# Dense products in column tiles, and score blocks outside score runs

## Chip, cores and metric

The kernel runs on one core of one Trainium2 chip. The metric is the device time of one execution in microseconds (us), given as the median of three runs. A core has TensorE (PE; its weight loads are shown as PEld), VectorE (DVE), ScalarE (ACT), GpSimd (POOL) and SyncE (SP), each with its own instruction queue; they wait for one another by semaphores. TensorE writes PSUM, which here holds eight banks of 128 partitions x 512 fp32.

## What is computed

```python
xn = layernorm(x)                                   # x: 2048 x 512, bf16
q = (xn @ wq).reshape(B, S, 32, 16).transpose(0, 2, 1, 3)
k, v = xn @ wk, xn @ wv                             # 16 wide, shared by all 32 heads
p = softmax(einsum("bhqd,bkd->bhqk", q, k) * 0.25)
s = (einsum("bhqk,bkd->bhqd", p, v) heads side by side) @ wo
g = silu(silu(xn @ w1) @ w2)                        # w1: 512 x 1792, w2: 1792 x 512
out = x + s * g
```

## The kernel before

The queries are cut into 4 chunks of 512, the heads into 8 groups of 4, the keys into 16 tiles of 128. So there are 32 groups in all (chunk by chunk), each with 16 key tiles of 4 rows, a row being one head. One row of one key tile is a **block**: scores of 128 keys x 512 queries, one PSUM bank. There are 2048.

**Scores** (`score`, `burst`, L523 to L544). A head has 16 dimensions, so TensorE is used in four row tiles of 32 partitions: up to four blocks are computed side by side, head i from partitions 32i. Keys lie in `kTa` for even groups, and shifted by 16 partitions in `kTb` for odd ones.

**Exponentials.** ScalarE takes two blocks at once from a double bank `psA` (`exp_A`, L560: 128x1024, then two rows of one key tile are done). VectorE takes single blocks, or a pair, from the banks D and D1 (`psD`) or F (`psF`): it makes an int16 that read as bf16 is a power of two (`exp_D`, L582). Three versions of it, shifted by constants, are averaged for accuracy; the other two come from GpSimd, which adds the constants for a whole tile of four blocks (`shift`, L607). The second buffer set for these lies in parts of `x_sb`.

**Attention times values** (`emit_PV`, L650). Here TensorE is used in four column tiles: a **quad** is four products with 128 keys to 32 outputs each, one per row of the group, into `psO`. A block of ScalarE needs one product, a block of VectorE three. At the end of a group VectorE normalises (`gn1` to `gn4`).

**Dense work** (`emit_job`, L901): q, the two layers of the gate (h and z), and the output product (w, and wp for the last chunk). It uses the whole array, 128x128 weights and 512 columns, always into `psF`. h and z go through a tanh on ScalarE (L939) and a product on VectorE (L971). For a token tile, z leaves the gate in `tmp_sb` (two sets of four); `w` multiplies it into `fin_sb` (L983), and `add` adds x into `ob_sb` (L950), which is stored.

**Order.** All engines' instructions are put in order by a planner when the kernel is built (the loop at L1180). It models each engine (`Sched.model`, L95): a product of 512 columns 0.216 us, a switch between row, column and full mode 0.104 us. It goes from **score run** to score run: a run is two blocks for ScalarE and, in the other two row tiles, blocks for VectorE if its banks are free (`score_run`, `fill_D`). `needed` is the latest start with which ScalarE won't wait, `release` the earliest. Between runs lies a gap with a number of slots of 0.216 us, each used for a quad or a dense product; if both stand in one gap, a slot is given up for the switch (L1218, L1220). Slots that stay empty can get products of zeros (`filler`, L917, and `warm`, L334) that keep TensorE's clock up, if its recent activity is below KEEP. Dense jobs have a fixed order by due time (`timed`, L766 to L773) and are paced by `behind`. Which blocks VectorE takes is not fixed: a key tile is opened for VectorE when a bank is free in a run and nothing else is open, and ScalarE takes what is left. The exponentials of ScalarE are as many as remain.

A tile for ScalarE takes rows 0, 1 in one run and 2, 3 in another; VectorE's blocks in a run are of the other two rows. VectorE's tiles are taken from a group's last key tiles. Finished exponentials of ScalarE lie in a ring of 11 buffers (`pa_sb`) until their products are done.

In `Sched`, `reads` and `writes` give the waits: whatever isn't done yet is waited for by a semaphore.

Of the kernel before, what the change touches and what calls it, by code (L numbers as in the profile page):

```python
# [13 lines left out]
P = 128  # L14
# [182 lines left out]
def bass_recurrent_scan__grouped_kv_mqa__dense_activation_silu__prompt_kernel(  # L197
# [33 lines left out]
    AGE2, AGE_ST, FIRST, FRONT_D, FRONT_K, SHORT, ST_EARLY, Q_ACT = 12.0, 1.5, 9.4, 1, 4, 0, 3, 1  # L231
    KEEP, ENDQ, ROUND, MAXJOB, AHEAD, Q_EARLY = 0.6, 12, 3.0, 2, 3, 0.20
    LEAD, LEAD_END, SLIP, AGE, AGE1, MARGIN = 3, 3, 0.2, 2.0, 1.2, 0.0
    HALF_LO, HALF_HI = 1, 3
    EV = "vava"
    PVWAIT = 0.2
    NF, F_FROM, F_LEFT, F_LATE, DENSE_END, HOLD, F_BEHIND = 14, 0.05, 9, 3, 0.95, 10, 0

    with ExitStack() as es:
# [13 lines left out]
        w2_sb = sb("w2_sb", [P, NFT, D])  # L253
        kT_sb = [sb("kTa_sb", [P, S]), sb("kTb_sb", [P, S])]
        vaug_sb = sb("vaug_sb", [P, 1 + NPH, NKT, 32])
        qT_sb = sb("qT_sb", [P, 2, NDC, NQ])
# [6 lines left out]
        t_sb = sb("t_sb", [P, 2, NQ])  # L263
        tmp_sb = sb("tmp_sb", [P, 2, 4, D])
        fin_sb = sb("fin_sb", [P, 2, D])
        ob_sb = sb("ob_sb", [P, NOB, D])
# [562 lines left out]
        def front_evac(tk):  # L829
# [36 lines left out]
        def emit_job(t, n):  # L866
# [31 lines left out]
            def f(e):  # L898
                for m in items:
                    l, r = pair(m)  # L900
                    h = e.matmul(ap, lhsT=l, rhs=r, start=(m == 0), stop=(m == end))  # L901
                return h
            op("pe", f, reads=rd, writes=[b], cost=("full", [None] * len(items), NQ))
            jst["part"] += len(items)
            if k != "wp":
                jst["slots"] += len(items)
            if jst["part"] == SIZE[k]:
# [3 lines left out]
                else:  # L911
                    task(k, evac, 0.69, jb=jb, bank=b, reads=[b], writes=[])
                if k in ("z", "w"):
# [3 lines left out]
        def filler(n):  # L917
            gi = state["g"]
            if gi < NGRP and K.pe_last >= gdone[gi] and all(npv[gi]):
                def f(e):  # L920
                    for _ in range(n):
                        r = e.matmul(psO[:, :], lhsT=zero_sb[:, 0:P], rhs=zero_sb[:, :], start=False, stop=False,
                                     skip_group_check=True)
                    return r
                op("pe", f, reads=["zero"], writes=["O"], cost=("full", [None] * n, NQ))
                return
# [29 lines left out]
        def add(tk):  # L956
            tt = tk["jb"][1]
            final_add("v", tt, fin_sb[:, tt % 2, :], ("fin", tt % 2))
            tok.add(("add", tt))

        def evac(tk):
# [3 lines left out]
            if k in ("h", "z"):  # L965
# [3 lines left out]
                else:  # L969
                    dst, key = tmp_sb[:, (jb[1] // 4) % 2, jb[1] % 4, :], ("tmp", jb[1] % 8)  # L970
                op("v", lambda e: e.scalar_tensor_tensor(out=dst, in0=t_sb[:, n % 2, :], scalar=1.0, in1=src,  # L971
# [9 lines left out]
            elif k == "w":  # L981
                tt = jb[1]
                op("v", lambda e: e.scalar_tensor_tensor(out=fin_sb[:, tt % 2, :], in0=src, scalar=0.25,  # L983
                                                         in1=tmp_sb[:, (tt // 4) % 2, tt % 4, :],
                                                         op0=ALU.mult, op1=ALU.mult),
                   reads=[b, ("tmp", tt % 8)], writes=[("fin", tt % 2)], cost=tk["cost"])
                tok.add(("wev", tt))
                task("add", add, 0.42, jb=jb, reads=[("fin", tt % 2), ("x", 12 + tt % 4)], writes=[])
            elif k == "wp":
# [71 lines left out]
        def v_cand():  # L1061
# [4 lines left out]
            if blks and may_D(blks):  # L1066
# [3 lines left out]
                if len(two) == 2 and (two[0]["bank"], two[1]["bank"]) == ("D", "D1") and two[0]["idx"] == two[1]["idx"] and may_D(two):  # L1070
                    d2 = max(tv, K.ready("v", ["D", "D1"], [ph_key(0, slot_of[b["idx"]], b["pos"]) for b in two]))
                    if d2 <= d + 0.1 and meets(d + 0.735) >= meets(d2 + 1.27):
                        d, blks = d2, two
# [41 lines left out]
        def score_run(t):  # L1115
# [18 lines left out]
            if second:  # L1134
                ast["tile"] = None

        def fill_D(t, free):
# [42 lines left out]
        while state["g"] < NGRP or front or jobs or jst["open"] or tasks:  # L1180
# [23 lines left out]
            if slots > 0:  # L1204
                gi = state["g"]
                full = blocked or sum(held(("pa", k)) for k in range(NPA)) >= HOLD
# [6 lines left out]
                can = job_ready(t) and not did  # L1213
                end = gi < NGRP and t >= gdone[gi] - PVWAIT and owed[gi] <= ENDQ
                dense_first = can and not full and not end and (jst["open"] or behind() or not more)
# [30 lines left out]
        half = [(slice(256 * h, 256 * h + 256), ("half", h)) for h in range(2)]  # L1246
        tmp = tmp_sb[:, (tt // 4) % 2, :, :]
        def resid(k, src, key, start):
# [32 lines left out]
        def gate(k):  # L1281
            bank, key = tail_bank(k)
            op("v", lambda e: e.scalar_tensor_tensor(out=fint_sb[:, k, :], in0=bank, scalar=0.25, in1=tmp[:, k, :],
                                                     op0=ALU.mult, op1=ALU.mult),
               reads=[key, ("tmp", (tt + k) % 8)], writes=[("spart", k)], cost=0.69)

        def gate_late(k):
            op("v", lambda e: e.tensor_tensor(fint_sb[:, k, :], fint_sb[:, k, :], tmp[:, k, :], ALU.mult),
               reads=[("spart", k), ("tmp", (tt + k) % 8)], writes=[("spart", k)], cost=0.42)

# [49 lines left out]
```

## Time and profile before

| what | us |
|---|---|
| median of 3 runs (lowest, highest) | 679.59 (679.39, 679.68) |
| profiled execution, its time | 679.43 |
| its span, first to last instruction | 677.6 |
| first exponential of ScalarE ends at | 11.74 |
| last exponential of ScalarE ends at | 668.54 |

A group line of the profile reads: line, engine, operation, output <- inputs, shapes, xcount, then busy time and mean ns of one, then the idle time in front of these instructions and what ended it. In the timeline a row has start, duration, engine, line, and in brackets the idle time before it. The granted clock of TensorE was 1.00 throughout. Instructions on ScalarE and VectorE overlap a little with the next one, so the distance of their ends, not their duration, is what one costs.

### The profile page before, as it was taken

The page shows a single profiled execution, that of the slowest core. Times are in us where ns is not written, and L with a number is a line of the kernel's source. Part 1 is how long each engine was busy: PE and PEld are TensorE (multiplying, and loading weights), DVE is VectorE, ACT ScalarE, POOL GpSimd, SP SyncE. Part 2 cuts the span into 40 slices and gives each one's busy share as a digit, 9 for nine tenths or more (in the row PEclk, how much of TensorE's full clock was granted, in tenths as well). Part 3 has the DMA queues.
Part 4 walks back from the last instruction along what each step waited for, and adds up shares of the span by engine and source line. Part 5 has one row for each costly group of instructions (what it writes and reads, how often), then busy time and mean ns, then how long its engine had stood idle before and what let it go on. Part 6 is the DMA issues. An engine that isn't in the chain of part 4 may idle for free.

```text
span 677.6 us, 14816 instructions
## 1 busy us (share of the span) xinstructions
PE 637.9 (94%) x6232; PEld 186.8 (28%) x6311; DVE 594.2 (88%) x994; ACT 664.0 (98%) x762; POOL 366.6 (54%) x371
## 2 busy tenths in 40 slices
PE   8999999999999999999999999999999999999997
PEld 4422222222222222222222222222222222222222
DVE  7888888888898879988898898998988889988997
ACT  6999999999999999999999999999999999999995
POOL 3154644644655646655565555646464646765563
PEclk9999999999999999999999999999999999999999
DMA  6340000000000001000000000000000000000100
GB/s 175 135 145 2 1 1 1 1 2 1 1 1 2 1 16 32 18 1 1 1 2 1 2 1 2 16 17 17 18 1 1 1 2 2 1 1 17 48 1 32
DMA packets 12322, 12.25 MB, mean 18 GB/s; under 512 B 2528, under 2 KB 11744, under 8 KB 12256
## 3 DMA queue, kind: packets, MB, share of 16 engines
q1 hardware_dynamic: 11680, 10.78, 5.1%
q8 instruction: 49, 0.80, 0.5%
q10 hardware_dynamic: 576, 0.52, 0.2%
q14 instruction: 17, 0.14, 0.1%
HBM read 8.95 MB, written 2.10 MB: 16 GB/s over the span
## 4 chain that ended last, share of the span: by engine, by line
ACT 89%; PE 4%; DVE 4%; issue 1%; POOL 1%; DMA 0%; POOLq 0%; SPq 0%
ACT pa_sb L560 84%; ACT t_sb L939 5%; PE psA L531 1%; PE psO L650 1%; DVE stats_sb L346 1%; DVE ph_sb L582 1%; DVE xn_sb L367 1%; PE psF L901 1%; DMA x_sb<-in_A_x_dram 0%; POOL ph_sb L607 0%; POOL rstd_sb L355 0%; PE psD L378 0%; DVE kTa_sb L421 0%; DVE x_sb L582 0%; PE psD L531 0%
## 5 line engine op out<-in xcount | busy, mean ns | idle before, releaser
L560 ACT ACTIVATE pa_sb<-psA 128x1024 bf16<-128x1024 f32 x677 | 641.2, 1177 | 1.7 <-PE psA L531 1.2
L607 POOL INT64_ADD ph_sb<-ph_sb x292 | 302.5, 1048 | 234.8 <-DVE ph_sb L582 234.7
L582 DVE TENSOR_SCALAR ph_sb<-psD 128x512 int16<-128x512 f32 x530 | 360.1, 690 | 52.4 <-PE psD L531 43.9
L650 PE MATMUL psO<-ph_sb,vaug_sb 128*32 128x512 bf16 x1758 | 211.7, 384 | 0.6 <-ACT pa_sb L560 0.3
L650 PE MATMUL psO<-pa_sb,vaug_sb 128*32 128x512 bf16 x1354 | 199.2, 384 | 0.0
L531 PE MATMUL psA<-qT_sb,kTa_sb 32*128 32x512 bf16 x688 | 133.5, 384 | 9.5 <-ACT pa_sb L560 6.2
L531 PE MATMUL psA<-qT_sb,kTb_sb 32*128 32x512 bf16 x666 | 129.2, 384 | 11.5 <-ACT pa_sb L560 9.5
L531 PE MATMUL psD<-qT_sb,kTb_sb 32*128 32x512 bf16 x323 | 118.2, 384 | 0.0
L531 PE MATMUL psD<-qT_sb,kTa_sb 32*128 32x512 bf16 x314 | 116.9, 384 | 0.4 <-DVE ph_sb L582 0.4
L607 POOL INT64_ADD x_sb<-x_sb x54 | 55.7, 1044 | 41.8 <-DVE x_sb L582 41.8
L582 DVE TENSOR_SCALAR x_sb<-psD 128x512 int16<-128x512 f32 (+1 forms) x96 | 66.9, 700 | 12.4 <-PE psD L531 11.7
L531 PEld LDWEIGHTS psA<-qT_sb,kTa_sb 32*128 32x128 bf16 x688 | 32.4, 90 | 140.1 <-ACT pa_sb L560 126.4
L531 PEld LDWEIGHTS psA<-qT_sb,kTb_sb 32*128 32x128 bf16 x666 | 31.3, 91 | 142.0 <-ACT pa_sb L560 132.3
L650 PEld LDWEIGHTS psO<-ph_sb,vaug_sb 128*32 128x32 bf16 x1758 | 53.6, 95 | 56.4 <-issue 37.0
L901 PE MATMUL psF<-xnT_sb,w_sb 128*128 128x512 bf16 x195 | 61.3, 384 | 3.4 <-issue 2.2
L901 PE MATMUL psF<-w_sb,u_sb 128*128 128x512 bf16 x208 | 62.5, 384 | 1.9 <-issue 1.4
L650 PEld LDWEIGHTS psO<-pa_sb,vaug_sb 128*32 128x32 bf16 x1354 | 50.1, 94 | 42.7 <-issue 31.0
L650 PE MATMUL psO<-x_sb,vaug_sb 128*32 128x512 bf16 x324 | 55.6, 384 | 0.0
L939 ACT ACTIVATE t_sb<-psF 128x512 bf16<-128x512 f32 x72 | 54.1, 752 | 0.0
L971 DVE SCALAR_TENSOR_TENSOR u_sb<-t_sb,psF 128x512 bf16<-128x512 bf16 x56 | 38.2, 682 | 7.0 <-ACT t_sb L939 6.4
L582 DVE TENSOR_SCALAR ph_sb<-psF 128x512 int16<-128x512 f32 x48 | 32.4, 676 | 0.0
L531 PEld LDWEIGHTS psD<-qT_sb,kTa_sb 32*128 32x128 bf16 x314 | 27.6, 91 | 2.0 <-DVE ph_sb L582 1.5
(107 smaller groups left out, 343.2 us busy)
## 6 DMA issues: line engine op xcount, KB each, us to landing
w_sb<-in_B_w_dram SPq DMA_DIRECT2D x2, 1792.0 KB, 8.3
x_sb<-in_A_x_dram SPq DMA_DIRECT2D x18, 128.0 KB, 2.2
out_dram<-ob_sb SPq DMA_DIRECT2D x14, 128.0 KB, 1.7
x_sb<-in_A_x_dram SPq DMA_DIRECT2D x3, 512.0 KB, 6.7
wop_sb<-in_A_wo_dram SPq DMA_DIRECT2D x1, 512.0 KB, 4.0
wq_sb<-in_A_wq_dram SPq DMA_DIRECT2D x1, 384.0 KB, 6.4
x_sb<-in_A_x_dram ACTq DMA_DIRECT2D x2, 128.0 KB, 3.0
kTb_sb<-kTa_sb SPq DMA_DIRECT2D x16, 16.0 KB, 1.8
```

Of the source, the lines that this page charges most:

```text
L346: op("v", lambda e: e.bn_stats(stats_sb[:, t, :], x_sb[:, t, :]), reads=[("x", t)], writes=[("st", t)], cost=0.687)
L367: op(eng, lambda e: e.tensor_scalar(xn_sb[:, t % 8, :], x_sb[:, t, :], mv_sb[:, t, 0:1], rstd_sb[:, t:t + 1], op0=ALU.subtract, op1=ALU.mult),
L531: return e.matmul(ap, lhsT=kT_sb[g % 2][32 * i:32 * i + 32, kt * P:(kt + 1) * P], rhs=qT_sb[32 * i:32 * i + 32, c % 2, g // 2, :], start=T ...
L560: d = op("a", lambda e: e.activation(pa_sb[:, sl, :], psA[k][:, :], ACT.Exp, scale=ESCALE), reads=["A%d" % k], writes=[("pa", sl)], cost=2 ...
L582: d = op("v", lambda e: e.tensor_scalar(ph_ap(0, sl, 512 * pos, 512 * pos + m), src, float(PH_ONE + PH_BIAS), 0.0, op0=ALU.add, op1=ALU.ma ...
L607: d = op("gp", lambda e, j=j: e.int64_add(ph_ap(j, sl, 0, 4 * NQ).bitcast(I64), ph_ap(0, sl, 0, 4 * NQ).bitcast(I64), PH_SHIFT[j] * 0x0001 ...
L650: r = e.matmul(psO[32 * i:32 * i + 32, :], lhsT=vaug_sb[:, p["v"], p["kt"], :], rhs=p["ap"], start=s0, stop=s1, tile_position=(0, 32 * i), ...
L901: h = e.matmul(ap, lhsT=l, rhs=r, start=(m == 0), stop=(m == end))
L939: op("a", lambda e: e.activation(t_sb[:, n % 2, :], bank_ap(b), ACT.Tanh, scale=0.5 if jb[0] == "h" else 0.25), reads=[b], writes=[("t", n ...
L971: op("v", lambda e: e.scalar_tensor_tensor(out=dst, in0=t_sb[:, n % 2, :], scalar=1.0, in1=src, op0=ALU.add, op1=ALU.mult), reads=tk["read ...
```

## The change

- **Dense products** are made of four products in column tiles (`columns`), each 128 rows by 32 outputs, to the same bank. The zero products into `psO` are too. In the planner they cost as much as before, and they are now in the same mode as the quads.
- **Masked keys**: a new tensor `km_sb` holds, for rows 2 and 3 (MI), both halves of the key layout and the last 6 key tiles (MK), the keys in that row's partitions and zeros in all others. GpSimd clears it, and SP's queue moves keys into it (`move_KM`, 8 transfers). A score block can then be computed as a product over all 128 rows in column mode, outside of a score run.
- **Filling**: `col_want` asks whether such a block would be at VectorE at least XGAIN = 0.6 us (in a leftover slot XLEFT = 0.5 us) earlier than by riding in the next run, and `col_fill` issues it. The loop that fills the gap asks for every slot anew, and gives no slot up between quads and dense products.
- **Buffers**: `tmp_sb` has one set of four, `fin_sb` is gone and `w` and `add` work in `ob_sb`. A z job therefore waits for the output product of the token tile four before, and the due times are clipped to that order.
- **Constants**: KEEP 0.6 to 0.65, Q_EARLY 0.20 to 0.18, AGE 2.0 to 2.5, DENSE_END 0.95 to 0.96.

```diff
+    MI, MK = (2, 3), 6
+    XHOLD, XGAIN, XLEFT, XBEH, PAIR = 8, 0.6, 0.5, 99, 1
+        km_sb = sb("km_sb", [P, 2, len(MI), MK * P])
-        tmp_sb = sb("tmp_sb", [P, 2, 4, D])
-        fin_sb = sb("fin_sb", [P, 2, D])
+        tmp_sb = sb("tmp_sb", [P, 4, D])
...
+        def columns(e, bank, lhsT, rhs, start, stop):
+            for i in range(4):
+                r = e.matmul(bank[32 * i:32 * i + 32, :], lhsT=lhsT[:, 32 * i:32 * i + 32], rhs=rhs, start=start, stop=stop,
+                             tile_position=(0, 32 * i), skip_group_check=True)
+            return r
...
+        def move_KM(c):
+            a = max(0, (NKT - MK) * P - c * NQ)
+            if a >= NQ:
+                return
+            d0 = c * NQ + a - (NKT - MK) * P
+            for p in range(2):
+                for m, i in enumerate(MI):
+                    op("sp", lambda e, p=p, m=m, i=i: e.dma_start(
+                        km_sb[32 * i + DH * p:32 * i + DH * p + DH, p, m, d0:d0 + NQ - a],
+                        kT_sb[0][32 * i:32 * i + DH, c * NQ + a:(c + 1) * NQ]),
+                       reads=[("kT", 0, 2 * c), ("kT", 0, 2 * c + 1)], writes=[("km", p, m, c)], lane=f"mm{c}{p}{m}")
...
         rstd_pow(1)
+        op("gp", lambda e: e.memset(km_sb[:], 0.0), writes=[("km", p, m, c) for p in range(2) for m in range(len(MI)) for c in range(NC)], cost=2.6)
...
+        when = {jb: x for x, jb in timed}
+        timed = [(min(x, when["z", jb[1] + 4] - 0.001) if jb[0] == "w" else x, jb) for x, jb in timed]
...
-                return all(("hev", c, ft) in tok for ft in range(NFT)) and (c < 2 or ("wev", jb[1] - 8) in tok) and \
+                return all(("hev", c, ft) in tok for ft in range(NFT)) and (c < 1 or ("wev", jb[1] - 4) in tok) and \
...
                     move_K(c)
+                    move_KM(c)
...
-                    h = e.matmul(ap, lhsT=l, rhs=r, start=(m == 0), stop=(m == end))
+                    h = columns(e, ap, l, r, m == 0, m == end)
...
-            op("pe", f, reads=rd, writes=[b], cost=("full", [None] * len(items), NQ))
+            op("pe", f, reads=rd, writes=[b], cost=("col", [0, 1, 2, 3] * len(items), NQ))
...
+        def col_pick(t):
+            for o in dst["open"]:
+                gi, kt = o["tile"]
+                for i in o["todo"]:
+                    if i in MI and kt >= NKT - MK and K.ready("pe", [("km", gi % 2, MI.index(i), kt // 4)]) <= t:
+                        return o, i
+            return None
+
+        def col_want(t, least):
+            if front or group_A() >= NGRP or sum(held(("pa", k)) for k in range(NPA)) >= XHOLD or (XBEH < 99 and behind(XBEH)):
+                return None
+            pick = col_pick(t)
+            if pick is None:
+                return None
+            vfree = K.free["v"] + 0.62 * len(dst["fifo"])
+            ride = needed() + 0.43
+            best = None
+            for b in BANKS:
+                if hold[b] is None and (b != "F" or not jobs or not next_job(t)):
+                    r = max(t, K.ready("pe", [], [b]))
+                    gain = ride - max(vfree, r + 0.43)
+                    if gain > least and (best is None or r < best[0]):
+                        best = (r, b) + pick
+            return best
+
+        def col_fill(w):
+            _, bank, o, i = w
...
+            def f(e):
+                return columns(e, bank_ap(bank), km_sb[:, g % 2, m, k0:k0 + P], qT_sb[:, c % 2, g // 2, :], True, True)
+            op("pe", f, reads=[("qT", c % 2, g // 2), "qTb", ("km", g % 2, m, kt // 4)], writes=[bank], cost=("col", [0, 1, 2, 3], NQ))
+            dst["fifo"].append(dict(tile=o["tile"], i=i, bank=bank, idx=idx, pos=pos, rows=o["rows"]))
...
-                if dense_first:
-                    did = emit_job(t, slots)
-                if slots - did >= (2 if did else 1):
-                    did += emit_PV(max(t, K.pe_last + K.pe_len) + 0.08, slots - did - (1 if did else 0))
-                if can and not dense_first and slots - did >= (2 if did else 1):
-                    did += emit_job(t, slots - did - (1 if did else 0))
+                while did < slots:
+                    t1 = t if not did else max(t, K.pe_next("col"))
+                    w = col_want(t1, XGAIN)
+                    part = slots - did
+                    if w is not None:
+                        k = int((w[0] - t1 - 0.05) / 0.2163 + 0.8)
+                        if k <= 0:
+                            did += col_fill(w)
+                            continue
+                        part = min(part, k)
...
+                    n = 0
+                    if dense_first:
+                        n = emit_job(t1, part)
+                    if not n:
+                        n = emit_PV(t1 + 0.08, part)
+                    if not n and can and not dense_first:
+                        n = emit_job(t1, part)
+                    if not n:
+                        w = col_want(t1, XLEFT)
+                        if w is not None and w[0] <= t1 + 0.1:
+                            n = col_fill(w)
+                        else:
+                            break
+                    did += n
```

More of the change, by code (lines that the diff above doesn't have):

```diff
@@ L231, in bass_recurrent_scan__grouped_kv_mqa__dense_activation_silu__prompt_kernel @@
     AGE2, AGE_ST, FIRST, FRONT_D, FRONT_K, SHORT, ST_EARLY, Q_ACT = 12.0, 1.5, 9.4, 1, 4, 0, 3, 1
-    KEEP, ENDQ, ROUND, MAXJOB, AHEAD, Q_EARLY = 0.6, 12, 3.0, 2, 3, 0.20
-    LEAD, LEAD_END, SLIP, AGE, AGE1, MARGIN = 3, 3, 0.2, 2.0, 1.2, 0.0
+    KEEP, ENDQ, ROUND, MAXJOB, AHEAD, Q_EARLY = 0.65, 12, 3.0, 2, 3, 0.18
+    LEAD, LEAD_END, SLIP, AGE, AGE1, MARGIN = 3, 3, 0.2, 2.5, 1.2, 0.0
     HALF_LO, HALF_HI = 1, 3
@@ L236, in bass_recurrent_scan__grouped_kv_mqa__dense_activation_silu__prompt_kernel @@
     PVWAIT = 0.2
-    NF, F_FROM, F_LEFT, F_LATE, DENSE_END, HOLD, F_BEHIND = 14, 0.05, 9, 3, 0.95, 10, 0
+    MI, MK = (2, 3), 6
+    XHOLD, XGAIN, XLEFT, XBEH, PAIR = 8, 0.6, 0.5, 99, 1
+    NF, F_FROM, F_LEFT, F_LATE, DENSE_END, HOLD, F_BEHIND = 14, 0.05, 9, 3, 0.96, 10, 0
     with ExitStack() as es:
@@ L911, in emit_job @@
                 else:
-                    task(k, evac, 0.69, jb=jb, bank=b, reads=[b], writes=[])
+                    task(k, evac, 0.69, jb=jb, bank=b, reads=[b], writes=[("ob", jb[1] % NOB)] if k == "w" else [])
                 if k in ("z", "w"):
@@ L921, in f @@
                     for _ in range(n):
-                        r = e.matmul(psO[:, :], lhsT=zero_sb[:, 0:P], rhs=zero_sb[:, :], start=False, stop=False,
-                                     skip_group_check=True)
+                        r = columns(e, psO, zero_sb[:, 0:P], zero_sb[:, :], False, False)
                     return r
-                op("pe", f, reads=["zero"], writes=["O"], cost=("full", [None] * n, NQ))
+                op("pe", f, reads=["zero"], writes=["O"], cost=("col", [0, 1, 2, 3] * n, NQ))
                 return
@@ L957, in add @@
             tt = tk["jb"][1]
-            final_add("v", tt, fin_sb[:, tt % 2, :], ("fin", tt % 2))
+            final_add("v", tt, ob_sb[:, tt % NOB, :], ("ob", tt % NOB))
             tok.add(("add", tt))
@@ L969, in evac @@
                 else:
-                    dst, key = tmp_sb[:, (jb[1] // 4) % 2, jb[1] % 4, :], ("tmp", jb[1] % 8)
+                    dst, key = tmp_sb[:, jb[1] % 4, :], ("tmp", jb[1] % 4)
                 op("v", lambda e: e.scalar_tensor_tensor(out=dst, in0=t_sb[:, n % 2, :], scalar=1.0, in1=src,
@@ L982, in evac @@
                 tt = jb[1]
[L983 to L986, printed above, removed]
+                op("v", lambda e: e.scalar_tensor_tensor(out=ob_sb[:, tt % NOB, :], in0=src, scalar=0.25,
+                                                         in1=tmp_sb[:, tt % 4, :], op0=ALU.mult, op1=ALU.mult),
+                   reads=[b, ("tmp", tt % 4)], writes=[("ob", tt % NOB)], cost=tk["cost"])
                 tok.add(("wev", tt))
-                task("add", add, 0.42, jb=jb, reads=[("fin", tt % 2), ("x", 12 + tt % 4)], writes=[])
+                task("add", add, 0.42, jb=jb, reads=[("ob", tt % NOB), ("x", 12 + tt % 4)], writes=[])
             elif k == "wp":
@@ L1071, in v_cand @@
                     d2 = max(tv, K.ready("v", ["D", "D1"], [ph_key(0, slot_of[b["idx"]], b["pos"]) for b in two]))
-                    if d2 <= d + 0.1 and meets(d + 0.735) >= meets(d2 + 1.27):
+                    if PAIR and d2 <= d + 0.1 and meets(d + 0.735) >= meets(d2 + 1.27):
                         d, blks = d2, two
@@ L1135, in score_run @@
                 ast["tile"] = None
+        def col_pick(t):
[23 more added lines that the diff above has]
+            _, bank, o, i = w
+            (gi, kt), idx = o["tile"], o["idx"]
+            c, g = gi // NG, gi % NG
+            pos = len(o["rows"]) - len(o["todo"])
+            o["todo"].remove(i)
+            if not o["todo"]:
+                dst["open"].remove(o)
+            m, k0 = MI.index(i), (kt - NKT + MK) * P
+            def f(e):
+                return columns(e, bank_ap(bank), km_sb[:, g % 2, m, k0:k0 + P], qT_sb[:, c % 2, g // 2, :], True, True)
+            op("pe", f, reads=[("qT", c % 2, g // 2), "qTb", ("km", g % 2, m, kt // 4)], writes=[bank], cost=("col", [0, 1, 2, 3], NQ))
+            dst["fifo"].append(dict(tile=o["tile"], i=i, bank=bank, idx=idx, pos=pos, rows=o["rows"]))
+            hold[bank] = "blk"
+            return 1
         def fill_D(t, free):
@@ L1204, in bass_recurrent_scan__grouped_kv_mqa__dense_activation_silu__prompt_kernel @@
             if slots > 0:
-                gi = state["g"]
-                full = blocked or sum(held(("pa", k)) for k in range(NPA)) >= HOLD
                 jb = next_front(t)
@@ L1212, in bass_recurrent_scan__grouped_kv_mqa__dense_activation_silu__prompt_kernel @@
                         did = 2
-                can = job_ready(t) and not did
-                end = gi < NGRP and t >= gdone[gi] - PVWAIT and owed[gi] <= ENDQ
-                dense_first = can and not full and not end and (jst["open"] or behind() or not more)
-                if dense_first:
-                    did = emit_job(t, slots)
-                if slots - did >= (2 if did else 1):
-                    did += emit_PV(max(t, K.pe_last + K.pe_len) + 0.08, slots - did - (1 if did else 0))
-                if can and not dense_first and slots - did >= (2 if did else 1):
-                    did += emit_job(t, slots - did - (1 if did else 0))
+                while did < slots:
[8 more added lines that the diff above has]
+                        part = min(part, k)
+                    full = blocked or sum(held(("pa", k)) for k in range(NPA)) >= HOLD
+                    can = job_ready(t1) and not (jb and did == 2 and False)
+                    gi = state["g"]
+                    end = gi < NGRP and t1 >= gdone[gi] - PVWAIT and owed[gi] <= ENDQ
+                    dense_first = can and not full and not end and (jst["open"] or behind() or not more)
+                    n = 0
[12 more added lines that the diff above has]
+                    did += n
             if more and not blocked:
@@ L1246, in bass_recurrent_scan__grouped_kv_mqa__dense_activation_silu__prompt_kernel @@
         half = [(slice(256 * h, 256 * h + 256), ("half", h)) for h in range(2)]
-        tmp = tmp_sb[:, (tt // 4) % 2, :, :]
+        tmp = tmp_sb[:, :, :]
         def resid(k, src, key, start):
@@ L1284, in gate @@
                                                      op0=ALU.mult, op1=ALU.mult),
-               reads=[key, ("tmp", (tt + k) % 8)], writes=[("spart", k)], cost=0.69)
+               reads=[key, ("tmp", (tt + k) % 4)], writes=[("spart", k)], cost=0.69)
         def gate_late(k):
             op("v", lambda e: e.tensor_tensor(fint_sb[:, k, :], fint_sb[:, k, :], tmp[:, k, :], ALU.mult),
-               reads=[("spart", k), ("tmp", (tt + k) % 8)], writes=[("spart", k)], cost=0.42)
+               reads=[("spart", k), ("tmp", (tt + k) % 4)], writes=[("spart", k)], cost=0.42)
         for k in (1, 3):
```

## Prediction

> **What bounds the kernel now.** I read the page's busy times first, then the chain that ended last, the groups, the waits, and last the timeline gap by gap. The page shows two nearly full engines:
>
> ```profile
> PE 637.9 (94%) x6232; PEld 186.8 (28%) x6311; DVE 594.2 (88%) x994; ACT 664.0 (98%) x762; POOL 366.6 (54%) x371
> ...
> ACT 89%; PE 4%; DVE 4%; issue 1%; POOL 1%; DMA 0%; POOLq 0%; SPq 0%
> ...
> L560 ACT ACTIVATE pa_sb<-psA 128x1024 bf16<-128x1024 f32 x677 | 641.2, 1177 | 1.7 <-PE psA L531 1.2
> ```
>
> ScalarE carries the chain, and in front of its 677 exponentials it idles 1.7 us in all. The chain of waits gives the price of each:
>
> ```profile
> 563.00 0.49 ACT t_sb L939
> 563.49 18.33 ACT pa_sb L560 x20
> ```
>
> Twenty exponentials in 18.33 us are 0.917 us each (the 1177 ns of the group includes overlap with the neighbour), a tanh is 0.49. In the timeline the first exponential ends at 11.74 us and the last at 668.54. So the span is 11.74 + 676 x 0.917 (619.9) + 72 x 0.49 (35.3) + 1.6 of stalls + 9.07 behind the last one = 677.6. The profiled execution took 679.43 us, 1.8 more than its span and 0.16 under the median of 679.59; sums below start from 679.43.
>
> There are 32 groups x 16 key tiles x 4 rows = 2048 score blocks of 128x512. One exponential takes two, so 677 take 1354, and VectorE has the other 694. **Only this split can move the end:** two blocks given to VectorE remove one exponential, 0.917 us. What keeps VectorE from more is in the waits (us in total, times, longest), the sum of the windows view over 30 to 667 us, and the timeline near 608 us:
>
> ```profile
> DVE ph_sb L582 <- PE psD L531: 43.9, 159, 1.1
> ...
> DVE x_sb L582 <- PE psD L531: 11.7, 43, 1.1
> ```
>
> ```profile
> sum 637.00, PE 605.88 PEld 172.29 DVE 562.85 ACT 636.49 POOL 356.50; mean PE 86.55 PEld 24.61 DVE 80.41 ACT 90.93 POOL 50.93
> ```
>
> ```profile
> 608.18 0.69 DVE L582 TENSOR_SCALAR x_sb<-psD 128x512 int16<-128x512 f32 x1 [0.18 <-PE psD L531]
> 609.04 0.69 DVE L582 TENSOR_SCALAR x_sb<-psD 128x512 int16<-128x512 f32 x1 [0.17 <-PE psD L531]
> 609.91 0.69 DVE L582 TENSOR_SCALAR x_sb<-psD 128x512 int16<-128x512 f32 x1 [0.17 <-PE psD L531]
> 610.99 0.69 DVE L582 TENSOR_SCALAR x_sb<-psD 128x512 int16<-128x512 f32 x1 [0.39 <-PE psD L531]
> ```
>
> The reader is to see that VectorE idles 637.0 - 562.9 = 74.2 us in the steady part, and 55.6 of that is waiting for a score block. One comes with each score run, and VectorE is done before the next. Back to back, such a block costs it 0.60 us from end to end, not 0.69.
>
> **Part 1, dense products in column tiles (the new helper, L901, L922).** 568 dense products (224 + 224 + 60 + 60 weight loads in the groups) become four products and four loads each. The nearest row is the attention-value quad of L650, the same form. In the timeline, successive quads start 0.215 to 0.227 us apart, and successive full products 0.215 to 0.227 as well; behind a score run the first quad starts after 0.321 us, the first full product after 0.323. So the edit costs 0 per product, and nothing is gained by itself: both stream 512 columns, so below nothing is excluded. The upper end is four loads one after another, 4 x 0.095 = 0.38 us, +0.154 each. I take 0, the quad's row.
>
> What it gives is a gap without a second switch: now only 16 of its 2,229 steps in the timeline go between dense and quad. TensorE's own time isn't on the chain, so I count 0 us here.
>
> [...] Here a 128x32 load takes 94 to 95 ns and a full 128x128 one 97, so four do cost more load time; the quads' spacing says that they are hidden. [...]
>
> **Part 2, VectorE's blocks filled outside score runs (the new picking, wanting and filling functions).** A fill is one quad slot, 0.216 to 0.227 us, where a block that rides in a run costs TensorE nothing. It is wanted when a bank is free, the block is of rows 2 or 3 and of the last six key tiles, and the planner sees VectorE served 0.6 us earlier (0.5 in a leftover slot) than by the next run. I put this test to the 650 gaps between score runs from 35 to 667 us, with the trace's times for bank, VectorE and ScalarE. It holds in 120: 60 of the 73 gaps that a tanh (0.49 us) or a stall makes longer, and 60 of the 577 others; the real advance is 0.63 us at the median. Two of a tile's four rows are allowed, and a block is taken away with every run, so I keep half: 60 fills. A fill's wait for its bank is new, and in TensorE's queue the next score run, and with it ScalarE, stands behind it; it costs nothing as long as VectorE reads the bank when the planner expects, as the 1.7 us of idle in front of L560 say of today's order.
>
> Not every fill adds a block: some only come before one that would have ridden, and later runs find a bank full. The ends are 0 net blocks and 45. The upper end is VectorE's room: a block costs 0.60 and shortens the span by 0.46, so 45 eat 45 x 1.06 = 48 of the 55.6 us. I take 24, two fifths of the 60, since the 78 gaps that now bring two blocks will often bring one. **24 blocks are 12 exponentials fewer: 12 x 0.917 = 11.0 us.**
>
> **What must hold.** TensorE: of those gaps 16 hold no slot of work and 138 one, and streaming and two switches of 0.104 leave 0.44 and 0.22 us in them, so 32 + 138 slots are free. Another 53 hold zero products (31 of L922; 19 on psD and 3 on psF of L337 beside the fixed 15 and 3). That is 223. The forecast needs 60 for fills, 24 x 2 / 4 = 12 for the two more products of each block, and 12 x 0.49 / 0.216 = 27 that go with 12 gaps: 99. If this cover is gone, a slot is 0.216 us on the chain. POOL gets 6 more tiles of 2.06 us at 54% busy. The wait ring: finished exponentials whose products haven't started number 3 at the median, 8 at most, against 11 buffers.
>
> **The small edits, each at 0.** The clearing of the masked keys on POOL is 3072 columns; the row of 128x2048 took 1.81 us, so an estimate of 2.7, from 20.8 us on, and POOL then idles 5.87 us until 26.6 for the next statistics. If that cover were gone, VectorE's normalising (waiting 0.9 us there) is late by as much. Eight 1.8 us moves enter SP's queue, in front of the loads of wo and w2; even one after another they are 14 us, and w2 is first used at 140 us, wo at 235. In the front they wait only for the key evictions that the moves before them wait for. One gate buffer instead of two puts the output product of a token tile before the gate of the tile four later. The trace has gates 12 to 15 at 563 to 614 us and output products 8 to 11 at 621 to 636, so these must swap; their last group of heads is exponentiated by about 505 us (three quarters of the way), 50 us before. The gate in place goes to a buffer stored over 100 us earlier. The changed constants (KEEP, Q_EARLY, AGE, DENSE_END) shift order within slack: between nothing and one block tile (1.8 us) either way, taken as 0.
>
> **The sum.** 679.43 - 11.0 = 668.4 us.
>
> **Rivals.**
> - *VectorE is filled nearly whole* (net 40 to 45 blocks: 18 to 23 us, 657 to 661). For it: 469 tanh-free gaps bring one block and idle 0.11 us each, a backlog would drain there. Against: half the rows aren't allowed, and 8.5 us of the idle waits for tanh. Chance 0.14.
> - *It hardly happens* (net 0 to 9 blocks: 675 to 679.4). A fill is bought for the latest ride, but VectorE's median wait is about 0.17 us, so fills mostly replace rides. For it: only 11 of its waits for blocks exceed 0.5 us. Chance 0.16; half of this is within 0.2%.
> - *TensorE becomes the bound, slower than before.* It decides from 223 slots. The place is the gap behind each run, the price 0.216 us per slot over, as a new wait of L560 for psA. With 280 slots wanted it would be +12 us, less the 0 to 5 that the exponentials give back: about 688, 682 to 700. If only the loads of part 1 came exposed, the point is 48 us / 568 = 0.085 us per product; at the full 0.154 it is 87 - 48 = 39 us over, 718. For it: TensorE shows 94% busy, and a fill is paid where a ride is free. Against: the free slots and the spacing of quads. Chance 0.16.
>
> **How the numbers follow.** Forecast 0.54 with its own range of 662 to 675 (net 10 to 38 blocks). Faster by over 0.2% (1.4 us, about what a measurement of this kernel can tell from no change): 0.54 + 0.14 + half of the second rival, 0.76; the same 0.08; slower 0.16. The range of 657 to 682 leaves out the slow rival and a sliver below, under 0.2.
>
> **What would show it.** Count L560: 665 is the forecast, 677 the second rival, under 658 the first. New score products of the form 128*32 on psD should number near 60; VectorE's wait for psD should fall from 55.6 to some 30 us. Part 1 is wrong if dense quads start over 0.25 us apart. The slow rival shows as idle time of L560 behind psA far above 1.7 us. I am wrong if exponentials fall and the span doesn't, or if the tail behind the last one grows past 9.07 us.

## The result, and the profile after

The changed kernel takes 687.20 us (median of 6 runs, 684.22 to 690.30), the kernel before 679.58 on the same chips. The ratio is 1.0108, with a 95% interval of 1.0084 to 1.0131: slower by 1.1%, where 668.4 us had been forecast. In the profile of the changed kernel TensorE's granted clock is 0.50 from 15.69 to 39.58 us, and by their mean clocks (0.975 to 0.990, 0.998 to 1.000 in the others) it was also halved for a while in 8 of the 80 later runs of the kernel before; that is the mechanism of this case, so it is told below.

The profiled execution took 688.93 us, its span 687.0. On its page:

```profile
PE 667.2 (97%) x8221; PEld 187.5 (27%) x8221; DVE 589.8 (86%) x968; ACT 664.0 (97%) x760; POOL 369.8 (54%) x374
...
PEclk9589999999999999999999999999999999999999
...
ACT 84%; PE 9%; DVE 2%; issue 2%; POOL 1%; DMA 1%; SPq 0%; POOLq 0%
...
L583 ACT ACTIVATE pa_sb<-psA 128x1024 bf16<-128x1024 f32 x675 | 643.2, 1191 | 11.2 <-PE psA L554 10.7
```

The reader is to see four things. The exponentials are 675, 2 fewer than before and not 12. The idle time in front of them has grown from 1.7 to 11.2 us. VectorE is no busier than before (589.8 us). And the second and third slice of the clock row are 5 and 8, where before every slice had a 9:

```profile
PEclk9999999999999999999999999999999999999999
```

The waits say the same (us in total, times, longest):

```profile
DVE ph_sb L605 <- PE psD L554: 54.0, 151, 1.5
...
ACT pa_sb L583 <- PE psA L554: 10.7, 14, 3.2
DVE x_sb L605 <- PE psD L554: 10.2, 30, 0.8
```

VectorE's wait for blocks hasn't fallen: 64.2 us, from 55.6. ScalarE waits 14 times for scores, up to 3.2 us. The sum closes: two exponentials fewer are -1.8; by the distances of their ends ScalarE's stalls rose from 1.9 to 13.1 us, +11.2, nearly all of it before 45 us; 679.4 - 1.8 + 11.2 = 688.8, against 688.93 measured. **So the loss lies in the first 45 us**, called the front below, in which x is still being normalised and transposed. The timeline shows where it begins:

```profile
13.13 2.66 POOL L520 MEMSET km_sb<- 128x3072 bf16 x1
13.19 3.70 DVE L376 TENSOR_SCALAR xn_sb<-x_sb,mv_sb,rstd_sb 128x512 bf16<-128x512 bf16 x4 [0.77 <-POOL rstd_sb L364]
...
13.22 0.39 PE L554 MATMUL psA<-qT_sb,kTa_sb 32*128 32x512 bf16 x2
...
16.30 1.03 PE L387 MATMUL psD<-ident,xn_sb 128*128 128x128 bf16 x8 [2.70 <-DVE xn_sb L376]
...
17.92 1.02 ACT L583 ACTIVATE pa_sb<-psA 128x1024 bf16<-128x1024 f32 x1 [3.25 <-PE psA L554]
```

The same place in the kernel before, where nothing stands between GpSimd's exponentiation of the statistics (`rstd_pow`) and the normalisings:

```profile
11.79 1.06 POOL L355 TENSOR_TENSOR rstd_sb<-rstd_sb,mhalf_sb 128x4 f32<-128x4 f32 x1
12.89 1.39 DVE L367 TENSOR_SCALAR xn_sb<-x_sb,mv_sb,rstd_sb 128x512 bf16<-128x512 bf16 x4 [0.77 <-POOL rstd_sb L355]
13.69 0.62 PE L378 MATMUL psD<-ident,xn_sb 128*128 128x128 bf16 x8 [0.34 <-DVE xn_sb L367]
```

Four normalisings of VectorE, 1.39 us before, take 3.70. The first of them alone lasts from 13.19 to 15.93 (2.74 us, otherwise 0.41): it ends 0.15 us behind GpSimd's clearing of the masked keys. TensorE, which waits for the normalised tiles, runs dry (has nothing ready to do) for 2.70 us, 0.34 before, and the windows view (window; length, then busy us of PE, PEld, DVE, ACT, POOL; granted clock, DMA share, GB/s) shows what follows:

```profile
8.00:12.00 4.00, 3.41 (x50) 2.30 (x48) 3.71 (x11) 3.28 (x7) 0.26 (x1) 1.00 0.78 252
12.00:16.00 4.00, 1.46 (x7) 0.40 (x7) 3.23 (x4) 2.62 (x3) 3.70 (x3) 0.96 0.10 26
16.00:24.00 8.00, 7.70 (x58) 3.60 (x62) 5.91 (x14) 4.09 (x4) 0.00 (x0) 0.50 0.65 230
24.00:32.00 8.00, 8.00 (x55) 2.92 (x54) 4.15 (x12) 5.52 (x7) 1.25 (x2) 0.50 0.03 7
32.00:40.00 8.00, 8.00 (x65) 2.25 (x63) 5.41 (x15) 5.74 (x6) 1.26 (x2) 0.53 0.05 12
40.00:48.00 8.00, 8.00 (x103) 3.35 (x101) 6.24 (x12) 7.68 (x9) 2.24 (x3) 1.00 0.28 78
```

Before, the window of 28 to 32 us was:

```profile
28.00:32.00 4.00, 3.69 (x34) 1.78 (x34) 3.98 (x9) 3.89 (x6) 0.00 (x0) 1.00 0.42 111
```

From 15.69 to 39.58 us the granted clock is 0.50. From 24 us on TensorE is busy all the time (8.00 of 8.00), and ScalarE, busy for 3.89 of 4.00 us before, idles for nearly a third of the time.

**Theory A:** GpSimd's clearing holds VectorE up; TensorE runs dry; its clock is halved; the exponentials wait. **Theory B:** the new order of TensorE's work (column tiles, fills, constants) does it, and the held-up VectorE adds only its 2.3 us. The forecast had 12 exponentials fewer, and 10 of them didn't come. For this there are two more theories: **the banks** (a fill takes a bank that the next run would have used), against **scarcity** (too few fills are wanted).

### The profile page after: what moved, and what is told of

It reads as the page before. It is cut to its first block, busy times and chain, and to the rows that moved or that the text cites. A ratio compares the mean times of both kernels' runs of the same rounds, so it can differ in the third digit from the quotient of the medians.

```text
span 687.0 us, 18712 instructions
## 1 busy us (share of the span) xinstructions
PE 667.2 (97%) x8221; PEld 187.5 (27%) x8221; DVE 589.8 (86%) x968; ACT 664.0 (97%) x760; POOL 369.8 (54%) x374
## 3 DMA queue, kind: packets, MB, share of 16 engines
q8 instruction: 64, 1.05, 0.6%
## 4 chain that ended last, share of the span: by engine, by line
ACT 84%; PE 9%; DVE 2%; issue 2%; POOL 1%; DMA 1%; SPq 0%; POOLq 0%
ACT pa_sb L583 79%; ACT t_sb L964 5%; PE psA L554 3%; PE psO L673 2%; PE psF L339 2%; DMA x_sb<-in_A_x_dram 1%; DVE ph_sb L605 1%; POOL ph_sb L630 1%; PE psD L387 1%; PE psD L418 1%; DVE xn_sb L376 0%; PE psO L339 0%; DVE stats_sb L355 0%; PE psD L554 0%; DVE ob_sb L1008 0%
## 5 line engine op out<-in xcount | busy, mean ns | idle before, releaser
L583 ACT ACTIVATE pa_sb<-psA 128x1024 bf16<-128x1024 f32 x675 | 643.2, 1191 | 11.2 <-PE psA L554 10.7
L630 POOL INT64_ADD ph_sb<-ph_sb x284 | 292.6, 1043 | 227.5 <-DVE ph_sb L605 227.4
L605 DVE TENSOR_SCALAR ph_sb<-psD 128x512 int16<-128x512 f32 (+1 forms) x492 | 343.1, 719 | 59.1 <-PE psD L554 54.0
L554 PE MATMUL psD<-qT_sb,kTb_sb 32*128 32x512 bf16 x316 | 98.8, 386 | 0.1
L630 POOL INT64_ADD x_sb<-x_sb x64 | 66.4, 1050 | 48.8 <-DVE x_sb L605 48.8
L554 PE MATMUL psD<-qT_sb,kTa_sb 32*128 32x512 bf16 x283 | 89.9, 384 | 0.0
L605 DVE TENSOR_SCALAR x_sb<-psD 128x512 int16<-128x512 f32 (+1 forms) x113 | 79.2, 711 | 11.3 <-PE psD L554 10.2
L339 PE MATMUL psF<-xnT_sb,w_sb 128*32 128x512 bf16 x896 | 70.9, 384 | 0.3 <-DVE ob_sb L1008 0.3
L673 PE MATMUL psO<-x_sb,vaug_sb 128*32 128x512 bf16 x384 | 70.2, 382 | 0.0
L339 PE MATMUL psF<-w_sb,u_sb 128*32 128x512 bf16 x896 | 69.7, 384 | 0.0
L554 PEld LDWEIGHTS psD<-qT_sb,kTb_sb 32*128 32x128 bf16 x316 | 23.8, 91 | 0.6 <-DVE ph_sb L605 0.4
```

The costliest lines, as they stand in the source:

```text
L339: r = e.matmul(bank[32 * i:32 * i + 32, :], lhsT=lhsT[:, 32 * i:32 * i + 32], rhs=rhs, start=start, stop=stop, tile_position=(0, 32 * i), ...
L554: return e.matmul(ap, lhsT=kT_sb[g % 2][32 * i:32 * i + 32, kt * P:(kt + 1) * P], rhs=qT_sb[32 * i:32 * i + 32, c % 2, g // 2, :], start=T ...
L583: d = op("a", lambda e: e.activation(pa_sb[:, sl, :], psA[k][:, :], ACT.Exp, scale=ESCALE), reads=["A%d" % k], writes=[("pa", sl)], cost=2 ...
L605: d = op("v", lambda e: e.tensor_scalar(ph_ap(0, sl, 512 * pos, 512 * pos + m), src, float(PH_ONE + PH_BIAS), 0.0, op0=ALU.add, op1=ALU.ma ...
L630: d = op("gp", lambda e, j=j: e.int64_add(ph_ap(j, sl, 0, 4 * NQ).bitcast(I64), ph_ap(0, sl, 0, 4 * NQ).bitcast(I64), PH_SHIFT[j] * 0x0001 ...
L673: r = e.matmul(psO[32 * i:32 * i + 32, :], lhsT=vaug_sb[:, p["v"], p["kt"], :], rhs=p["ap"], start=s0, stop=s1, tile_position=(0, 32 * i), ...
```

## Experiments: the clearing

**The clearing elsewhere** (e1), in the changed kernel:

```diff
+        op("gp", lambda e: e.memset(km_sb[:], 0.0), reads=[("xnT", 0, 2)], writes=[("km", p, m, c) for p in range(2) for m in range(len(MI)) for c in range(NC)], cost=2.6)
         for t in range(4, 4 + ST_EARLY):
             stats(t)
...
         rstd_pow(1)
-        op("gp", lambda e: e.memset(km_sb[:], 0.0), writes=[("km", p, m, c) for p in range(2) for m in range(len(MI)) for c in range(NC)], cost=2.6)
```

> The changed kernel with one line moved: GpSimd clears the masked keys right after VectorE has copied the third transposed tile, near 8.7 us, where VectorE only runs its statistics, instead of next to its normalising near 13.2 us. It has 675 exponentials, 2 fewer than before. Theory A (the clearing holds up VectorE's normalising, TensorE then runs dry and its clock is halved for 11 to 29 us): the first normalising takes 0.41 us instead of 2.74, the clock stays at 1.00, and the time is 679.6 - 2 x 0.917 = 677.7 us, the 11 us of idle in front of the exponentials are gone. Theory B (the new order of TensorE's work, its column tiles or the changed constants starve the clock gate or ScalarE): no more than the 2.3 us of the held-up VectorE come back, 684 to 688 us, clock still below 1.00.

Measured: 678.45 us. The same kernel was run again, for a profile in which the clock isn't halved (e12):

> The same kernel as e1_clear_free, once more, for a profile in which TensorE's clock isn't halved in the front by chance, and for a closer ratio: 678.4 us, 0.998 of the kernel before, span 676.3, idle time in front of the exponentials about 2 us, clock 1.00.

678.43 us, ratio 0.9992 (0.9971 to 1.0012; for e1 0.9984, 0.9967 to 1.0001). Two of 12 runs each had a halved clock, which makes the intervals wide; the other 20 all lie between 677.9 and 679.3. In the timeline of e12, GpSimd clears from 8.72 to 11.38 us (2.66 us) beside VectorE's statistics, and

```profile
12.87 1.39 DVE L376 TENSOR_SCALAR xn_sb<-x_sb,mv_sb,rstd_sb 128x512 bf16<-128x512 bf16 x4 [0.77 <-POOL rstd_sb L364]
12.94 0.39 PE L554 MATMUL psA<-qT_sb,kTa_sb 32*128 32x512 bf16 x2
13.66 0.62 PE L387 MATMUL psD<-ident,xn_sb 128*128 128x128 bf16 x8 [0.34 <-DVE xn_sb L376]
```

The normalising is back at 1.39 us, TensorE's gap at 0.34, as before the change. Theory A's 677.7 is missed by 0.7 us; theory B's 684 to 688 is out.

**The clearing alone** (e2), in the kernel before, with nothing else of the change:

```diff
         rstd_pow(1)
+        op("gp", lambda e: e.memset(u_sb[:, 0, 0:6, :], 0.0), writes=[("u", 0, ft) for ft in range(6)], cost=2.6)
         mm_K(0, psO, "O", P, NQ)
```

> The kernel before, with nothing of the change but a clearing of as many columns (3072, of a buffer that is written much later) at the place where the change has it. 677 exponentials. Theory A: the first normalising takes some 2.7 us, TensorE's clock drops near 16 us, and the time is that of the changed kernel plus its 2 exponentials, 686 to 692 us. Theory B: the clearing alone costs at most the 2.3 us for which VectorE is held up, 679.6 to 682 us, clock 1.00.

Measured: 690.36 us, ratio 1.0152 (1.0130 to 1.0174), the clock halved in all 6 runs (mean 0.980 to 0.983).

```profile
13.06 3.70 DVE L367 TENSOR_SCALAR xn_sb<-x_sb,mv_sb,rstd_sb 128x512 bf16<-128x512 bf16 x4 [0.77 <-POOL rstd_sb L355]
16.17 1.03 PE L378 MATMUL psD<-ident,xn_sb 128*128 128x128 bf16 x8 [2.65 <-DVE xn_sb L367]
```

One instruction that GpSimd does in 2.66 us costs 10.8 us. That is shown, not argued: nothing else differs, and VectorE's and ScalarE's instructions come in the same order as before.

**Smaller clearings** (e10 with 1536 columns, e11 with 512; `0:6` becomes `0:3` and `0:1`):

> The kernel before with a clearing of 1536 columns, half of that of e2_before_clear, at the same place. 677 exponentials. If GpSimd holds VectorE's normalising for as long as the clearing lasts: the first normalising takes some 1.4 us and TensorE runs dry for 1.0 us less than the 1.3 that the whole clearing... the wait is then about 1.0 us. If the halved clock comes only when TensorE is idle for long enough, this one keeps 1.00 and costs about 1 us: 680.6 us. If any hold-up drops the clock: 686 us or more, as with the whole clearing (690.4).

> The kernel before with a clearing of 512 columns (a sixth) at the same place. 677 exponentials. Held for as long as the clearing lasts, the first normalising takes some 0.5 us instead of 0.41 and nothing else changes: 679.6 us, clock 1.00. If GpSimd's mere presence there cost more (a fixed price): over 681 us.

The durations are of the profiled run of each kernel; the last column is the median of its runs at the full clock.

| clearing | first normalising | TensorE dry | clock halved | runs at full clock, us |
|---|---|---|---|---|
| none (before) | 0.41 us | 0.34 us | 8 of 80 | 679.6 |
| 512 columns, 0.53 us | 0.61 | 0.52 | 3 of 10 | 679.7 |
| 1536 columns, 1.38 us | 1.46 | 1.37 | 8 of 10 | 680.5 |
| 3072 columns, 2.66 us | 2.7 | 2.65 | 6 of 6 | none |

The mean clock is 0.975 to 0.992 in the runs counted as halved and 0.998 to 1.000 in the others. The hold-up grows with the clearing. With the clock full it costs about its own length: the half clearing makes the normalising 1.05 us longer and the kernel 0.9 us. Whether the clock falls differs from run to run of one kernel, and the odds rise with the gap: 8 of 10 and 6 of 6 are far from 8 of 80, while 3 of 10 by itself isn't clear of it. The median of e10, 688.69 us, is neither of the two numbers expected of it, since its runs are a mixture of both cases.

The gap isn't all that decides. In the profile of e1 (683.05 us, mean clock 0.988) the clock is halved from 13.44 us on, though the gap there is only 0.33 us and had begun 0.2 us earlier. So the odds were not nothing before the change either, and what else in the front counts isn't shown.

**The hold-up without the halved clock** (e6): the changed kernel, clearing in place, and zero products to fill TensorE's gap:

```diff
             if k == "T":
+                if jb == ("T", 1, 0):
+                    def wf(e):
+                        for _ in range(13):
+                            r = e.matmul(ap, lhsT=zero_sb[:, 0:P], rhs=zero_sb[:, :], start=True, stop=True)
+                        return r
+                    op("pe", wf, reads=["zero"], writes=[b], cost=("full", [None], 1))
                 transposes(c, jb[2], ap, b)
```

> The changed kernel with the clearing left where it is, next to VectorE's normalising, and 13 zero products (2.8 us of TensorE) put in front of the transposes that wait for that normalising; the planner isn't told of them. 675 exponentials. Theory A in two parts (VectorE held up for 2.3 us, and TensorE's clock halved since it then ran dry): the first normalising still takes 2.7 us and the exponential behind it still waits some 3 us, but the clock stays at 1.00: 678.4 + 3 = 681 us. If the halved clock had another cause, 685 to 690 us as the changed kernel.

Measured: 680.21 us, mean clock 0.998 to 1.000 in 10 of 10. The timeline has GpSimd (2.66 us) and VectorE (3.70 us) as slow as in the changed kernel, ScalarE waiting nearly as long, and TensorE busy in between:

```profile
13.42 2.98 PE L848 MATMUL psD<-zero_sb 128*128 128x512 bf16 x13
16.24 0.61 PE L387 MATMUL psD<-ident,xn_sb 128*128 128x128 bf16 x8
...
17.21 1.02 ACT L583 ACTIVATE pa_sb<-psA 128x1024 bf16<-128x1024 f32 x1 [2.58 <-PE psA L554]
```

So the hold-up is worth 1.8 us (680.2 against 678.4), and the halved clock the other 4 to 10 of the changed kernel's six runs.

**The clearing on VectorE** (e9), in its own queue before x arrives:

```diff
+        op("v", lambda e: e.memset(km_sb[:], 0.0), writes=[("km", p, m, c) for p in range(2) for m in range(len(MI)) for c in range(NC)], cost=1.6)
         op("gp", lambda e: e.memset(kT_sb[1][:], 0.0), writes=[("kT", 1, c, i) for c in range(2 * NC) for i in range(4)])
...
-        op("gp", lambda e: e.memset(km_sb[:], 0.0), writes=[("km", p, m, c) for p in range(2) for m in range(len(MI)) for c in range(NC)], cost=2.6)
```

> The changed kernel with the clearing of the masked keys moved to VectorE's own queue, ahead of its first statistics, while it waits for the first rows of x (some 1.6 us by its row of 0.27 us for 256 words). 675 exponentials. Theory A: as the first kernel of this study, clock at 1.00, 678.4 us, at most 0.5 more if the first statistics start late; the best version of the change so far. Theory B is out already; a rival left is that the changed kernel's order drops the clock by itself now and then, then the median is above 679.6.

Measured: 678.41 us, ratio 0.9977 (0.9965 to 0.9990), no halved clock in 12 runs (mean 0.999 to 1.000). One run took 1347.92 us, unexplained; the other 11 lie between 678.2 and 678.8. The clearing takes VectorE 1.34 us from 1.68 us on, where it waits for x until 3.3. This is the only version whose interval lies wholly below 1, by 0.2%: the change without its accident.

## Experiments: columns, fills and banks

**Column tiles alone** (e3): the kernel before in its own order, its dense products issued by `columns`.

```diff
-                    h = e.matmul(ap, lhsT=l, rhs=r, start=(m == 0), stop=(m == end))
+                    h = columns(e, ap, l, r, m == 0, m == end)
```

> The kernel before, in its own order, with nothing of the change but the form of the dense products: each of 568 as four products in column tiles. 677 exponentials. Prediction's step (a product in columns costs the same 0.22 us): 679.6 us, within 0.5. Rival (the four weight loads come exposed at up to 0.154 us each): the spacing of dense products goes to 0.30 us or more and exponentials wait for psA, 690 us or more.

Measured: 679.51 us against 679.58, ratio 0.9987 (0.9961 to 1.0014). The groups have 896 products and 896 loads in place of 224:

```profile
L337 PE MATMUL psF<-xnT_sb,w_sb 128*32 128x512 bf16 x896 | 69.6, 384 | 0.0
...
L337 PEld LDWEIGHTS psF<-xnT_sb,w_sb 128*32 128x32 bf16 x896 | 16.3, 94 | 28.4 <-issue 21.5 <-DVE ph_sb L589 2.5 <-DVE u_sb L978 1.0
```

The products take 384 ns each as before, the loads 94 ns. Successive dense quads start 0.215 to 0.227 us apart, as the whole products do in the kernel before, so the loads are hidden.

**No fills** (e4): e1 with XGAIN and XLEFT at 99.

> The first kernel of this set (clearing moved) with the two gains set so high that no block is ever filled outside a score run. The planner then leaves ScalarE 679 exponentials instead of 675. If exponentials alone set the time: 679.6 + 2 x 0.917 = 681.4 us, 3.7 more than with the 47 fills. So the fills' whole worth would be 4 exponentials, 0.08 each, where the prediction had 12 for 60. If the fills also cost something elsewhere (waits of score runs behind them), the difference is under 3.7 us.

Measured: 682.85 us (1.0049, 1.0033 to 1.0065), 4.4 more than e1. The spans of the profiles of e4 and e12 differ by 4.0 us: 3.7 for the exponentials, 0.8 for stalls (3.2 against 2.4 us), less 0.4 in the tail behind the last exponential.

This run also shows what the rest of the change does without any fill: 2 exponentials more than the kernel before and 3.3 us longer. So the 47 fills bring 8 blocks and 4.4 us, and the rest (the new order of the slots, the single gate buffer, the constants) takes 4 blocks and 3.3 us away. Which part of the rest does that was not tried, but the column form by itself costs nothing (e3).

**More fills** (e5): both gains at 0.4.

> The first kernel of this study (clearing moved) with both gains lowered from 0.6 and 0.5 to 0.4 us, so that more blocks are filled outside score runs. The planner leaves ScalarE 683 exponentials, 8 more than with the higher gains. Theory of the banks (a fill takes one of the two banks that the next run would have used, so it replaces a ride): many more fills than 47, most next runs without a block for VectorE, and 678.4 + 8 x 0.917 = 685.8 us. Theory of scarcity (too few fills were wanted): more fills give VectorE more blocks; that the exponentials rise already speaks against it, and then the time should stay at or below 678.4 us all the same.

Measured: 687.58 us (1.0119, 1.0104 to 1.0133). That is 1.8 above the 685.8 of the banks' theory; ScalarE's stalls are 4.8 us in the profile, against 2.4 in e12.

**Two banks only** (e7), the kernel before with F kept from blocks:

```diff
-            banks = sorted(free_banks(t + SLIP), key=lambda b: (b == "F", K.ready("pe", [], [b])))
+            banks = sorted([q for q in free_banks(t + SLIP) if front or q != "F"], key=lambda b: (b == "F", K.ready("pe", [], [b])))
```

> The kernel before, in which VectorE's blocks may no longer use the third bank (F) once the front is over; they have only the two banks D and D1. Nothing else is changed. The planner leaves 695 exponentials, 18 more, that is 36 blocks fewer on VectorE, where 57 had ridden in F. Theory of the banks: VectorE's share hangs on free banks at the moment of a run; the time is 679.6 + 18 x 0.917 = 696.1 us, VectorE's wait for psD rises by 15 us or more. If banks were not what holds VectorE, the blocks would have moved to the other two and the time would be 679.6.

Measured: 695.32 us (1.0231, 1.0215 to 1.0247), and on its page and in its waits

```profile
L560 ACT ACTIVATE pa_sb<-psA 128x1024 bf16<-128x1024 f32 x695 | 659.6, 1200 | 1.3 <-PE psA L531 1.2
```

```profile
DVE ph_sb L582 <- PE psD L531: 79.8, 274, 1.0
```

One bank of three, used by only 57 blocks, was worth 36 blocks and 15.7 us. A ride is a block for VectorE in a score run. Counted in the timelines from 45 to 665 us (the exponentials over the whole run):

| kernel | exponentials | rides | fills | runs without a ride |
|---|---|---|---|---|
| before | 677 | 674 | 0 | 40 of 637 |
| e4 (clearing moved, no fills) | 679 | 670 | 0 | 87 of 636 |
| e12 (clearing moved) | 675 | 634 | 47 | 151 of 637 |
| e5 (more fills) | 683 | 583 | 73 | 228 of 636 |
| e7 (two banks) | 695 | 626 | 0 | 66 of 638 |

From e4 to e12, 47 fills come in and 36 rides go. Of the 47 runs that follow a fill in e12, 31 have no block for VectorE, two thirds, where without fills it is 87 of 636, a seventh. The timeline of e12 shows one such place:

```profile
86.11 0.40 PE L339 MATMUL psD<-qT_sb,km_sb 128*32 128x512 bf16 x4
...
86.77 1.16 DVE L605 TENSOR_SCALAR x_sb<-psD 128x1024 int16<-128x1024 f32 x1
...
86.95 0.39 PE L554 MATMUL psA<-qT_sb,kTb_sb 32*128 32x512 bf16 x2
...
87.86 0.39 PE L554 MATMUL psA<-qT_sb,kTb_sb 32*128 32x512 bf16 x2
...
88.18 0.40 PE L339 MATMUL psD<-qT_sb,km_sb 128*32 128x512 bf16 x4
```

The fill at 86.11 gives VectorE a pair, which it reads until 87.93. Both D banks are taken meanwhile, the runs at 86.95 and 87.86 carry only ScalarE's two blocks, and the next block for VectorE is again a fill. So a fill mostly brings forward a block whose bank the next run then lacks. In 19 of the 31 places both D banks were still taken when the run began, counting from a block's weight load to the end of VectorE's read; over all runs of the stretch this holds for 158 of 637 in e12, 94 of 636 in e4 and 45 of 637 before. In the other 12 one D bank was free, and why nothing rode there isn't shown. Scarcity is out: 73 fills gave fewer blocks than 47, not more.

**Another constant instead of fills** (e8): e4 with KEEP at 0.70.

> As the kernel without fills (e4_no_fills), with one constant changed: KEEP 0.65 to 0.70, the activity below which empty slots get zero products. No block is filled outside a run, and the planner happens to leave 675 exponentials, as many as the change with its 47 fills. If the fills' worth is no more than the scatter of the planner's order: 678.4 us, the same as e1_clear_free within 0.5, 1 to 2 under the kernel before. If fills give something beyond the number of exponentials: slower than 678.4 by over 1 us.

This run told less than it was meant to: the kernel has 677 exponentials, not the 675 of the expectation. It took 681.64 us (1.0031, 1.0018 to 1.0044), 2.1 more than the kernel before with as many exponentials; its stalls are 3.8 us against 1.9. One constant moved the planner by 2 exponentials, half of the fills' whole worth. That the planner's scatter is as large as the fills' worth is not shown.

## Why the prediction was wrong

- **What bounds the kernel: right.** The end follows ScalarE's exponentials at 0.917 us: 18 more gave +15.7 us in e7 (16.5 worked out), 2 fewer -1.2 in e12 (-1.8).
- **Part 1, a dense product in columns at +0: right.** e3 measured -0.1 us for all 568. The rival of exposed loads is out.
- **Part 2, 60 fills: right in size** (47). **24 net blocks from them: wrong.** The step that failed is "I take 24, two fifths of the 60". Against the same kernel without fills (e4, 690 blocks on VectorE) the 47 fills bring 8 net blocks, a sixth of them, and 4.4 us instead of 11.0. "Later runs find a bank full" was named and priced far too low; 31 of 47 next runs took no block. The second rival ("it hardly happens", 0 to 9 net blocks) is what happened to this part, with a reason close to the one given. Its neighbour has a slip in its sum: 45 blocks are 20.6 us, not 23; nothing hung on it.
- **The small edits of the order "between nothing and one block tile (1.8 us) either way, taken as 0": too small.** Without fills and with the clearing moved the change costs 3.3 us (e4), of which 1.8 are two exponentials; so of the kernel's 698 blocks against 694 only 4 are left.
- **What must hold: right.** TensorE had room; with the clearing moved, ScalarE waits 1.8 us in front of its exponentials. The slow rival, TensorE running out of slots, didn't occur; the kernel is slower by another mechanism.
- **The clearing "at 0": wrong, and it decided the sign.** The step failed twice. It was placed at 20.8 us, behind GpSimd's second exponentiation of statistics, but the line stands behind the first, which ends at 12.85 us in the trace of before; the four normalisings start 0.04 us later. And its cover was sought on GpSimd alone (5.87 us idle) when VectorE was the one to pay: "late by as much" was written only for a late start. Four normalisings start at 20.80 us too, so the place alone would not have saved this step. It was priced at 0 and measured at 10.8 us in the kernel before (e2) and 8.8 in the changed one (687.20 against 678.43). That TensorE's clock could be halved behind a gap of 2.70 us wasn't considered at all, though the clock row of before was known.
- How long the hold-up is, the traces show: the first normalising takes 2.74, 1.46 and 0.61 us beside clearings of 2.66, 1.38 and 0.53 us, and 0.41 us without one. VectorE's statistics weren't held: beside the clearing of e12 they took 676 to 684 ns, and the mean of all 16 is 680 ns there and 682 ns in the kernel before. Why the normalising is held and the statistics aren't isn't shown.

The miss adds up from these three: 668.4 forecast, 8.8 for the clearing, 6.6 that the fills bring less, and 3.3 for the rest of the order are 687.1, against 687.20 measured. With the accident repaired the change is worth 1.2 us (0.2%), not 11.0.

## What to carry to other kernels

A cover has to be sought on the other engines too, not only on the one that does the moved work: here a clearing of 2.66 us, which GpSimd did while it had nothing else to do, held one normalising of VectorE for 2.74 us. A short gap that starves TensorE is priced not by its own length alone but also by the halved clock that may follow, here 4 to 13 us, times the odds of it, here 8 of 10 runs at a gap of 1.37 us. And before more work is fed to a waiting engine, count the buffers through which it is fed: what is filled earlier through the same two banks takes the place of what would have come. A change of several parts needs a run with each of them left out before its gain is put down to one.

## What the runs showed of the hardware

- The halved clock had no one length: 10.24, 13.65, 23.89 and 34.13 us in the profiles of e10, e1, e2 and e11, whose mean clocks are 0.992, 0.988, 0.982 and 0.975. It differs between runs of one kernel too: the six mean clocks of the changed kernel go from 0.979 to 0.992. A gap of TensorE of 2.65 us (e2) went with a halved clock in 6 of 6 runs, one of 1.37 us (e10) in 8 of 10.
- A busy TensorE didn't bring the full clock back at once: in the changed kernel it stayed at 0.50 for 23.89 us, with TensorE at 8.00 of 8.00 us in the windows from 24 us on, and in e11 for 34.13 us. What ends the halved stretch isn't shown.
- One run of e8 took 821 us (mean clock 0.656), one of e9 1348 us (mean clock 1.00). Both are single and unexplained; the medians don't hang on them.
